# Chunk attention and a GELU layer on one core: the second tile's V loaded before the end of w_out, attention work moved into the first tile's second product, and tiles that DMA fills placed on multiples of 64 bytes

## The chip, the cores and the metric

The kernel runs on one core of a Trainium2 chip. The metric is the device time of one execution in microseconds (us). TensorE (PE) multiplies, VectorE (DVE), ScalarE (ACT) and GpSimd (POOL) do the elementwise work, and SyncE (SP) issues nearly all DMA transfers, in program order. Each engine takes its own instructions in the order in which the program lists them, and waits on semaphores for the others.

## The reference

```python
# q, k, v: (8 batches, 8 heads, 576 positions, 64); chunks of 64 positions, 9 per sequence
scores = scale * np.matmul(q_c, k_c.transpose(0, 1, 2, 4, 3))   # 64 x 64 in each chunk
attn = np.exp(scores - max); attn = attn / (attn.sum(-1) + 1e-9)
x = np.matmul(attn, v_c)            # regrouped to (4608 tokens, 512)
h = x @ w_in                        # 512 -> 2048
g = 0.5 * h * (1.0 + erf(h / sqrt(2)))
out = g @ w_out                     # 2048 -> 512, float32
```

The two products with w_in and w_out are nearly all of the arithmetic. Attention only looks within chunks of 64 positions.

## The kernel before, in words

The tokens are cut into nine tiles of 512. Tile t below 8 is the first eight chunks of batch t, and tile 8 collects the ninth chunk of every batch. For each tile there is an attention part, which gives x (128 x 4 x 512, bf16), a first product with w_in, 16 slots of four matmuls each (mm1_slot, or mm1_first for a tile's first four slots at once), each followed by Gelu on ScalarE, and a second product with w_out, 64 matmuls in blocks (phase). Everything is in bf16 with sums in float32, and the weights stay in SBUF.

The order of the work is written out by hand; nothing reorders it. From tile 2 on, q and k are transposed by DMA and the attention of tile t+1 is woven into the second product of tile t. Tiles 0 and 1 are different, because their data and the weights are still arriving: there PE transposes q and k (att_T), att_S makes the scores and their exponentials, att_av multiplies with V (a column of ones beside V gives the sum of the exponentials) and divides on DVE, and att_x transposes the result, which ScalarE or DVE copies into x. The four head pairs g of a tile go through these steps one by one.

Tile 0's second product runs by rows (mm2_rows): block f adds the products of row block f of w_out to all four output blocks, so it can start while the rest of w_out is on its way. Before the change, blocks 0 to 11 run so, and slots 12 to 15 then finish one output block each, with the last four row blocks of w_out. Tile 1's att_T and att_S stand in blocks 2 to 10, two of its att_av and one att_x in slots 14 and 15, and the other two att_av and three att_x within mm1_first of tile 1.

All loads go through one ring of seven float32 staging tiles (the tag "stage", 1 MB each) and are cast to bf16 on POOL, DVE or ScalarE. SP issues them in this order: q and k of tile 0 in eight pieces, V of tile 0 (four transfers in runs of 256 bytes), w_in in seven pieces, w_out's first quarter, q of tile 1, w_out's second quarter, k of tile 1, w_out's third and last quarters, V of tile 1 (four transfers), then q, k and V of tile 2. A quarter of w_out is four row blocks. PSUM has eight banks in three pools: mm (3), tp (2) and at (3).

The small tile act_scratch (128 x 1, float32) lies last in the pool of constants, ahead of the staging tiles; it takes a slot of 32 bytes, and in the built program the first staging tile begins at byte 59,040 of each partition, 32 past a multiple of 64. All staging tiles, the tiles of q, k and x, h and the output tiles stand at the same remainder.

Of the kernel before, what the change touches and what calls it, by code (L numbers as in the profile page):

```python
# [11 lines left out]
def kernel(  # L12
# [9 lines left out]
    nc = tc.nc  # L22
    P = 128
    f32 = mybir.dt.float32
    bf16 = mybir.dt.bfloat16
    Act = mybir.ActivationFunctionType

    B, H, S, D = q.shape
# [4 lines left out]
    G = H // 2  # L33
# [7 lines left out]
    FF = d_ff // P  # L41
    scale = 1.0 / (D ** 0.5)
# [34 lines left out]
    tiles = [dict() for _ in range(NT)]  # L77
# [51 lines left out]
    def load_v(t):  # L129
        raw = stage_tile()[:].rearrange("p (h n d) -> p h n d", h=H, d=D)  # L130
        tiles[t]["vf"] = raw
        rows_128(t, v, raw, False)

    def cast_qk(t, nm, g, copy):
        st = tiles[t]
        if t > 1 and nm == "k":
            copy(st[nm][:, :, g], st[nm + "f"][:, :, g].rearrange("p (q r) d -> p q r d", r=2))  # L137
            return
        copy(st[nm][:, g].rearrange("p j r d -> p r j d"), st[nm + "f"][:, 2 * g:2 * g + 2])  # L139

    def cast_v(t, n, copy):
        copy(v_rows[t][:, :, n, 0:D], tiles[t]["vf"][:, :, n])
# [123 lines left out]
            u = slice(half * (gs[0] % 2), half * (gs[-1] % 2 + 1))  # L266
            nc.scalar.activation(st["pT", 2 * g2 + r][:, u], st["s", g2][r][:, u], Act.Exp, scale=scale)

    def att_av(t, g, banks):

        st = tiles[t]
        half = CT // 2
        av = [pool.tile([P, half, D + 1], f32, tag=tag, name="av_ps") for pool, tag in banks]
        for n in range(half):
            for r in range(2):
                for c in range(2):
                    cs = slice(CH * c, CH * (c + 1))
                    nc.tensor.matmul(av[r][cs, n, :], st["pT", 2 * (g // 2) + r][cs, half * (g % 2) + n, :],  # L278
                                     v_rows[t][cs, 2 * g + r, n, 0:D + 1], start=True, stop=True,
                                     tile_position=(CH * c, CH * c))  # L280
        xn = work.tile([P, half, 2, D], bf16, tag="xn", name="xn", bufs=4)
        st["xn", g] = xn
        for r in range(2):
            rr = work.tile([P, half, 1], f32, tag="rr", name="rr", bufs=4)
            nc.vector.reciprocal(rr[:], av[r][:, :, D:D + 1])
            nc.vector.tensor_tensor(xn[:, :, r], av[r][:, :, 0:D], rr[:].to_broadcast([P, half, D]),  # L286
                                    op=mybir.AluOpType.mult)

    def att_x(t, g, copy, pool, tag):
        tp = pool.tile([P, CT // 2, P], bf16, tag=tag, name="tp")  # L290
        for n in range(CT // 2):
            nc.tensor.transpose(tp[:, n], tiles[t]["xn", g][:, n].rearrange("p r d -> p (r d)"), ident[:])  # L292
        copy(tiles[t]["x"][:, g, :], tp[:].rearrange("p n q -> p (n q)"))  # L293
# [4 lines left out]
    def mm1_first(t, banks, steps):  # L298
        st = tiles[t]
        st["h"] = hpool.tile([P, FF, MT], bf16, tag="h", name="h")  # L300
        h_ps = {}
        for step in steps:
            if callable(step):
                step()
                continue
            fs, kss = step
            for ks in kss:
                for f in fs:
                    if ks == 0:
                        pool, tag = banks[f]  # L310
                        h_ps[f] = pool.tile([P, MT], f32, tag=tag, name="h_ps")
                    nc.tensor.matmul(h_ps[f][:], w_in_sb[:, ks, f * P:(f + 1) * P], st["x"][:, ks, :],  # L312
                                     start=(ks == 0), stop=(ks == KS - 1))
        for f in range(len(banks)):
            nc.scalar.activation(st["h"][:, f, :], h_ps[f][:], Act.Gelu)
# [33 lines left out]
    def rows_out(t, ms):  # L349
        y_ps = tiles[t]["y_ps", ms]  # L350
        y_sb = ypool.tile([P, d_model], f32, tag="y", name="y_sb")
        (AC if t == 0 or ms < 3 and t + 1 < NT else DV)(y_sb[:], y_ps[:])  # L352
        if t == 0:
            held.append((ms, y_sb))
        elif t < B:
            store(t, ms, y_sb)
        else:
            for c in range(P // CH):
                m0 = (ms * (P // CH) + c) * S + MT
                nc.sync.dma_start(out[m0:m0 + CH, :], y_sb[c * CH:(c + 1) * CH, :])  # L360

    def last_rows(t, ms):
        h = d_model // 2
        for a, (pool, tag) in enumerate(((ps_mm, "mm"), (ps_at, "at"))):
# [6 lines left out]
            for c in range(P // CH):  # L371
                m0 = (ms * (P // CH) + c) * S + MT
                (nc.sync if c == 0 else nc.scalar).dma_start(
                    out[m0:m0 + CH, a * h:(a + 1) * h], y_sb[c * CH:(c + 1) * CH, :])

    def mm2_rows(t, f):

        last = MT // P - 1
        if f == 0:
            order = [(last, 0), (0, 0), (1, 0)]  # L380
        elif f == 1:
            order = [(last, 1), (0, 1), (1, 1), (2, 0), (2, 1)]
        else:
            order = [(ms, f) for ms in range(MT // P)]
        for ms, fi in order:
            if fi == 0:
                pool, tag = (ps_at, "at") if ms == last else (ps_mm, "mm")
                tiles[t]["y_ps", ms] = pool.tile([P, d_model], f32, tag=tag, name="y_ps")
            nc.tensor.matmul(tiles[t]["y_ps", ms][:], tiles[t]["h"][:, fi, ms * P:(ms + 1) * P], w_out_sb[:, fi, :],  # L389
                             start=(fi == 0), stop=False)  # L390

    def phase(t, extra2, by_rows=False, first=0):
        nms = MT // P
        order = [(ms, qt) for ms in range(nms) for qt in range(NQ)]
        if by_rows:
            order = [(None, f) for f in range(FF - FC)] + [(ms, NQ - 1) for ms in range(nms)]
        for f in range(first, FF):
            mm1_slot(t, f)
        for s, (ms, qt) in enumerate(order):
            for u in extra2.get(s, ()):  # L400
                u()
            if ms is None:
                mm2_rows(t, qt)
            else:
                mm2_slot(t, ms, qt)

# [16 lines left out]
            copy(w_in_sb[:, :, c * WC + i * P:c * WC + (i + 1) * P], raw[:, :, i * P:(i + 1) * P])  # L423
        return cast

    def load_w_out(c):
        raw = stage_tile()[:].rearrange("p (f n) -> p f n", f=FC)
        nc.sync.dma_start(raw, w_out_v[:, c * FC:(c + 1) * FC, :])

        def cast(i, copy):  # L430
            copy(w_out_sb[:, c * FC + i, :], raw[:, i, :])  # L431
        return cast
# [8 lines left out]
        for _ in range(n):  # L441
            nc.tensor.matmul(warm[:], rest[:, 0:P], rest[:], start=True, stop=True)

    act_scratch = consts.tile([P, 1], f32, name="act_scratch")

    def act_table(func):
        nc.scalar.activation(act_scratch[:], rest[:, 0:1], func)  # L447

    with tc.manual_schedule():
        for g in range(G):  # L450
# [7 lines left out]
        tp, at, mm = (ps_tp, "tp"), (ps_at, "at"), (ps_mm, "mm")  # L458
        for g in range(G - 1):
            cast_qk(0, "k", g, PO)  # L460
        cast_v(0, 0, PO)
        cast_qk(0, "k", G - 1, PO)
        cast_v(0, 1, PO)
        cast_v(0, 2, PO)
        for i in range(FC):
# [25 lines left out]
        att_x(0, 0, AC, *mm)  # L491
        att_av(0, 2, (at, tp))
        att_x(0, 1, AC, *mm)
        mm1_first(0, (mm, at, at, tp),
                  (((0, 1), (0,)), lambda: att_av(0, 3, (tp, at)), lambda: att_x(0, 2, AC, *mm),
                   ((0, 1), (1,)), lambda: act_table(Act.Gelu), lambda: att_x(0, 3, DV, *mm),
                   ((0, 1), (2,)), ((2, 3), (0, 1, 2)), ((0, 1, 2, 3), (3,))))
        win.append(load_w_in(NWC - 1))
        wout = [load_w_out(0)]
        load_qk(1, "q")  # L500
# [1 line left out]
        for c in range(1, NWC):  # L502
            for i in range(4):
                win[c](i, DV if i % 2 == 0 else PO)
            if c == 1:
                load_qk(1, "k")
            else:
                wout.append(load_w_out(c))
        for i in range(FC):
            wout[0](i, DV if i % 2 == 0 else PO)  # L510
        load_v(1)
        for g in range(G):
            cast_qk(1, "q", g, DV if g == 0 else PO)
        for i in range(FC):
# [2 lines left out]
            cast_qk(1, "k", g, DV if g % 2 == 0 else PO)  # L517
        for i in range(FC):
            wout[2](i, PO)
        for i in range(2):  # L520
            wout[3](i, PO)
        for n in range(CT // 2):
            cast_v(1, n, PO)

        def next_qk():
            for nm in "qk":
# [2 lines left out]
        Tq = [lambda g=g: att_T(1, "q", g, AC) for g in range(G)]  # L529
        Tk = [lambda g=g: att_T(1, "k", g, (AC, DV)[g % 2]) for g in range(G)]  # L530
        phase(0, {0: [lambda: act_table(Act.Exp)], 2: Tq[0:1], 3: Tq[1:2], 4: Tq[2:4], 7: Tk[0:2], 8: Tk[2:4],
                  9: [lambda: att_S(1, (0, 1)), next_qk], 10: [lambda: att_S(1, (2, 3)), lambda: wout[3](2, DV)],
                  11: [lambda: wout[3](3, AC)], 14: [lambda: att_av(1, 0, (at, at))],
                  15: [lambda: att_av(1, 1, (tp, tp)), lambda: att_x(1, 0, AC, *mm)]},
              by_rows=True, first=4)
        pool_cast_qk(2)
        every = (0, 1, 2, 3)
        mm1_first(1, (mm, mm, at, at),
                  (lambda: att_av(1, 2, (at, at)), (every, (0,)), lambda: att_x(1, 1, AC, *mm),
                   lambda: att_av(1, 3, (tp, tp)), (every, (1,)), lambda: att_x(1, 2, AC, *mm),  # L540
                   lambda: act_table(Act.Gelu), (every, (2,)), lambda: att_x(1, 3, DV, *tp), (every, (3,))))
        for t in range(1, NT):
            nxt = t + 1 < NT
            if nxt:
# [52 lines left out]
```

## Time and profile before

| | us |
|---|---|
| median of three runs | 294.69 (294.62 to 295.0) |
| the profiled execution's own time | 292.79 |
| its span, first to last instruction | 291.0 |
| PE busy | 277.8 (95% of the span) |
| ScalarE / DVE / POOL busy | 171.6 / 103.4 / 72.1 |
| start of tile 1's regular mm1 slots in the chain of waits | 59.01 |
| one of tiles 2 to 7, from first slot to first slot | 29.18 |

The chain of waits follows the work that ended last back to the start. It lies on PE for 91% of the span; what is not PE in it stands within the first 59 us. From there on a tile follows a tile every 29.18 us (113.90, 143.10, 172.27 and 201.44 in the chain) with PE hardly pausing.

### The profile page before, as it was taken

The page shows a single profiled execution, that of the slowest core. Times are in us where ns is not written, and L with a number is a line of the kernel's source. Part 1 is how long each engine was busy: PE and PEld are TensorE (multiplying, and loading weights), DVE is VectorE, ACT ScalarE, POOL GpSimd, SP SyncE. Part 2 cuts the span into 40 slices and gives each one's busy share as a digit, 9 for nine tenths or more (in the row PEclk, how much of TensorE's full clock was granted, in tenths as well). Part 3 has the DMA queues.
Part 4 walks back from the last instruction along what each step waited for, and adds up shares of the span by engine and source line. Part 5 has one row for each costly group of instructions (what it writes and reads, how often), then busy time and mean ns, then how long its engine had stood idle before and what let it go on. Part 6 is the DMA issues. An engine that isn't in the chain of part 4 may idle for free.

```text
span 291.0 us, 5942 instructions
## 1 busy us (share of the span) xinstructions
PE 277.8 (95%) x2401; PEld 134.2 (46%) x2431; DVE 103.4 (36%) x211; ACT 171.6 (59%) x347; POOL 72.1 (25%) x114
## 2 busy tenths in 40 slices
PE   7589999799999999999999999999999999999995
PEld 3354454444444444444444444444444444444444
DVE  2473242400940094009400950095009500950011
ACT  2547745588647864686468646864686468646400
POOL 2445565611431341053005300530006020000000
PEclk9969999999999999999999999999999999999999
DMA  7999999998879984995499539953999493030033
GB/s 235 253 346 377 364 354 240 192 237 227 221 203 222 263 181 145 215 254 113 143 212 255 116 141 207 254 124 140 197 136 146 91 235 75 2 136 8 0 74 72
DMA packets 119307, 53.87 MB, mean 185 GB/s; under 512 B 97648, under 2 KB 112240, under 8 KB 119280
## 3 DMA queue, kind: packets, MB, share of 16 engines
q1 hardware_dynamic: 119120, 53.36, 75.9%
q8 instruction: 19, 0.31, 0.5%
q10 hardware_dynamic: 160, 0.13, 0.2%
q14 instruction: 8, 0.07, 0.1%
HBM read 36.70 MB, written 9.44 MB: 159 GB/s over the span
## 4 chain that ended last, share of the span: by engine, by line
PE 91%; SPq 3%; DMA 2%; DVE 1%; issue 1%; ACT 1%
PE h_ps L323 40%; PE y_ps L338 38%; PE y_ps L389 3%; PE h_ps L312 3%; PE av_ps L236 2%; PE s_ps L184 2%; DMA arrival<-in_v_dram 2%; SPq L100 2%; SPq L90 1%; PE y_ps L367 1%; PE tp L292 1%; PE av_ps L278 1%; PE tp L148 1%; DVE xn L286 1%; ACT x L293 0%
## 5 line engine op out<-in xcount | busy, mean ns | idle before, releaser
L323 PE MATMUL h_ps<-x,w_in_sb 128*128 128x512 bf16 x535 | 118.4, 379 | 0.5
L325 ACT ACTIVATE h<-h_ps 128x512 bf16<-128x512 f32 x136 | 81.0, 598 | 59.3 <-PE h_ps L323 59.3
L338 PE MATMUL y_ps<-w_out_sb,h 128*128 128x512 bf16 x496 | 111.4, 379 | 1.5 <-issue 1.1
L323 PEld LDWEIGHTS <-w_in_sb 128*128 128x128 bf16 x544 | 53.2, 98 | 64.2
L338 PEld LDWEIGHTS <-h 128*128 128x128 bf16 x512 | 48.8, 98 | 57.4
L202 DVE STREAM_TRANSPOSE pt<-pT 128x256 f32<-128x256 f32 x28 | 12.2, 437 | 108.6 <-ACT pT L191 108.6
L139 POOL CAST q_nat<-arrival 128x512 bf16<-128x512 f32 x31 | 18.0, 621 | 96.2 <-DMA arrival<-in_q_dram 63.5
L162 POOL CAST v_nat<-arrival 128x1024 bf16<-128x1024 f32 x14 | 14.5, 1040 | 39.9 <-DMA arrival<-in_v_dram 30.6
L447 ACT ACT_TABLE_LOAD x18 | 23.1, 1283 | 1.0 <-PEq L581 0.7
L215 ACT COPY part<-part 32x32 f32<-32x32 f32 x56 | 12.3, 219 | 15.1 <-DVE part L205 14.6
L243 DVE TENSOR_TENSOR x<-av_ps,rc 128x512 bf16<-128x512 f32 x28 | 18.9, 676 | 2.2
L205 DVE TENSOR_REDUCE part<-pt 128x16 f32<-128x512 bf16 x28 | 19.2, 686 | 1.0
L352 DVE COPY y_sb<-y_ps 128x512 f32<-128x512 f32 x10 | 6.9, 691 | 34.9 <-PE y_ps L338 34.9
L137 POOL CAST k_nat<-arrival 128x512 bf16<-128x512 f32 x28 | 16.6, 613 | 5.8 <-DMA arrival<-in_k_dram 5.6
L352 ACT COPY y_sb<-y_ps 128x512 f32<-128x512 f32 x25 | 14.5, 580 | 3.3 <-PE y_ps L338 2.4
L191 ACT ACTIVATE pT<-s_ps 128x512 bf16<-128x512 f32 x28 | 14.3, 593 | 0.0
L389 PE MATMUL y_ps<-w_out_sb,h 128*128 128x512 bf16 x46 | 11.6, 380 | 0.1
L312 PE MATMUL h_ps<-x,w_in_sb 128*128 128x512 bf16 x30 | 8.6, 403 | 1.5 <-ACT x L293 1.0
L229 DVE STREAM_TRANSPOSE rc<-rb 128x512 f32<-128x512 f32 x14 | 9.9, 707 | 0.2
L229 DVE STREAM_TRANSPOSE rc<-across 128x512 f32<-128x512 f32 x14 | 9.8, 702 | 0.0
L423 POOL CAST w_in_sb<-arrival 128x512 bf16<-128x512 f32 x10 | 7.1, 729 | 7.6 <-DMA arrival<-in_moe_w_in_dram 7.6
L431 POOL CAST w_out_sb<-arrival 128x512 bf16<-128x512 f32 x10 | 6.9, 727 | 4.0 <-DMA arrival<-in_moe_w_out_dram 4.0
(52 smaller groups left out, 140.8 us busy)
## 6 DMA issues: line engine op xcount, KB each, us to landing
out_dram<-y_sb SPq DMA_DIRECT2D x32, 256.0 KB, 2.4
arrival<-in_k_dram SPq DMA_DIRECT2D x28, 256.0 KB, 6.5
arrival<-in_q_dram SPq DMA_DIRECT2D x7, 1024.0 KB, 6.8
arrival<-in_v_dram SPq DMA_DIRECT2D x42, 128.0 KB, 3.1
arrival<-in_moe_w_out_dram SPq DMA_DIRECT2D x4, 1024.0 KB, 14.1
arrival<-in_moe_w_in_dram SPq DMA_DIRECT2D x6, 512.0 KB, 8.0
arrival<-in_v_dram SPq DMA_DIRECT2D x8, 256.0 KB, 6.7
arrival<-in_v_dram SPq DMA_DIRECT2D x28, 64.0 KB, 2.7
```

What stands on the lines that cost most here:

```text
L137: copy(st[nm][:, :, g], st[nm + "f"][:, :, g].rearrange("p (q r) d -> p q r d", r=2))
L139: copy(st[nm][:, g].rearrange("p j r d -> p r j d"), st[nm + "f"][:, 2 * g:2 * g + 2])
L205: nc.vector.tensor_reduce(st["part", g2][:, c, :, :, 0], pt[:].rearrange("p n e u -> p n u e"), axis=mybir.AxisListType.X, op=mybir.AluOpT ...
L229: nc.vector.transpose(rc[:], tiles[t]["rb", g2][c].to_broadcast([P, NB, 32]))
L243: nc.vector.tensor_tensor(x.rearrange("p n (e u) -> p n e u", u=2), st["av"][g2][c][:].rearrange("p n (e u) -> p n e u", u=2), st["rc", 2 ...
L312: nc.tensor.matmul(h_ps[f][:], w_in_sb[:, ks, f * P:(f + 1) * P], st["x"][:, ks, :], start=(ks == 0), stop=(ks == KS - 1))
L323: nc.tensor.matmul(h_ps[:], w_in_sb[:, ks, f * P:(f + 1) * P], st["x"][:, ks, :], start=(ks == 0), stop=(ks == KS - 1))
L325: nc.scalar.activation(st["h"][:, f, :], h_ps[:], Act.Gelu)
L338: nc.tensor.matmul(y_ps[:], st["h"][:, f, ms * P:(ms + 1) * P], w_out_sb[:, f, :], start=(f == 0), stop=(f == FF - 1))
L352: (AC if t == 0 or ms < 3 and t + 1 < NT else DV)(y_sb[:], y_ps[:])
L389: nc.tensor.matmul(tiles[t]["y_ps", ms][:], tiles[t]["h"][:, fi, ms * P:(ms + 1) * P], w_out_sb[:, fi, :], start=(fi == 0), stop=False)
L447: nc.scalar.activation(act_scratch[:], rest[:, 0:1], func)
```

## The change

It has these parts.

- act_scratch becomes 128 x 32 float32, so that the first staging tile begins at byte 59,136, a multiple of 64, and all that follows it likewise. The reciprocals rr of one att_av share one tile.
- At the start, POOL casts the last piece of k of tile 0 ahead of the first piece of V, not behind it.
- Tile 0's last att_av (g = 3) stands before mm1_first, not within it, and its second multiply, one DVE instruction before, becomes four ScalarE instructions with a scale per partition.
- V of tile 1 is loaded ahead of w_out's last quarter, and that quarter comes in two halves. Its four casts go to DVE (12), POOL (13 and 15, behind the V casts) and ScalarE (14).
- Tile 0's second product runs by rows up to block 13; four short blocks 14 to 17 of two matmuls finish the output blocks. Tile 1's four att_av stand at blocks 12, 13, 15 and 17 and two of its att_x at 14 and 15; two att_x stay in mm1_first, which works by all four slots at once, over other PSUM banks. The copies of tile 0's third and fourth output blocks move into mm1_first.

```diff
-    def att_av(t, g, banks):
+    def att_av(t, g, banks, second=None):
...
+        rr = work.tile([P, 2, half, 1], f32, tag="rr", name="rr", bufs=4)
         for r in range(2):
-            rr = work.tile([P, half, 1], f32, tag="rr", name="rr", bufs=4)
-            nc.vector.reciprocal(rr[:], av[r][:, :, D:D + 1])
-            nc.vector.tensor_tensor(xn[:, :, r], av[r][:, :, 0:D], rr[:].to_broadcast([P, half, D]),
-                                    op=mybir.AluOpType.mult)
+            nc.vector.reciprocal(rr[:, r], av[r][:, :, D:D + 1])
+            if r == 0 or second is None:
+                nc.vector.tensor_tensor(xn[:, :, r], av[r][:, :, 0:D], rr[:, r].to_broadcast([P, half, D]),
+                                        op=mybir.AluOpType.mult)
+            else:
+                for n in range(half):
+                    nc.scalar.activation(xn[:, n, r], av[r][:, n, 0:D], Act.Copy, scale=rr[:, r, n])
...
+    FR = FF - 2
+
+    def mm2_last(t, ms):
+        y_ps = tiles[t]["y_ps", ms]
+        for f in range(FR, FF):
+            nc.tensor.matmul(y_ps[:], tiles[t]["h"][:, f, ms * P:(ms + 1) * P], w_out_sb[:, f, :],
+                             start=False, stop=(f == FF - 1))
+        if ms < 2:
+            rows_out(t, ms)
...
-            order = [(None, f) for f in range(FF - FC)] + [(ms, NQ - 1) for ms in range(nms)]
+            order = [(None, f) for f in range(FR)] + [(ms, None) for ms in range(nms)]
...
-    def load_w_out(c):
+    def load_w_out(c, parts=1):
...
+        n = FC // parts
+        for a in range(parts):
+            nc.sync.dma_start(raw[:, a * n:(a + 1) * n], w_out_v[:, c * FC + a * n:c * FC + (a + 1) * n, :])
...
-    act_scratch = consts.tile([P, 1], f32, name="act_scratch")
+    act_scratch = consts.tile([P, 32], f32, name="act_scratch")
...
-        cast_v(0, 0, PO)
         cast_qk(0, "k", G - 1, PO)
+        cast_v(0, 0, PO)
...
+        att_av(0, 3, (tp, at), AC)
         mm1_first(0, (mm, at, at, tp),
-                  (((0, 1), (0,)), lambda: att_av(0, 3, (tp, at)), lambda: att_x(0, 2, AC, *mm),
-                   ((0, 1), (1,)), lambda: act_table(Act.Gelu), lambda: att_x(0, 3, DV, *mm),
-                   ((0, 1), (2,)), ((2, 3), (0, 1, 2)), ((0, 1, 2, 3), (3,))))
+                  (((0, 1), (0,)), lambda: att_x(0, 2, AC, *mm), ((0, 1), (1,)), lambda: act_table(Act.Gelu),
+                   lambda: att_x(0, 3, DV, *mm), ((0, 1), (2,)), ((2, 3), (0, 1, 2)), ((0, 1, 2, 3), (3,))))
...
-                wout.append(load_w_out(c))
+                if c == NWC - 1:
+                    load_v(1)
+                wout.append(load_w_out(c, 2 if c == NWC - 1 else 1))
...
-        load_v(1)
...
-        for i in range(2):
-            wout[3](i, PO)
         for n in range(CT // 2):
             cast_v(1, n, PO)
+        for i in (1, 3):
+            wout[3](i, PO)
...
-                  9: [lambda: att_S(1, (0, 1)), next_qk], 10: [lambda: att_S(1, (2, 3)), lambda: wout[3](2, DV)],
-                  11: [lambda: wout[3](3, AC)], 14: [lambda: att_av(1, 0, (at, at))],
-                  15: [lambda: att_av(1, 1, (tp, tp)), lambda: att_x(1, 0, AC, *mm)]},
+                  9: [lambda: att_S(1, (0, 1)), next_qk], 10: [lambda: att_S(1, (2, 3)), lambda: wout[3](0, DV)],
+                  12: [lambda: att_av(1, 0, (at, at))], 13: [lambda: att_av(1, 1, (tp, tp)), lambda: wout[3](2, AC)],
+                  14: [lambda: att_x(1, 0, AC, *at)],
+                  15: [lambda: att_av(1, 2, (at, tp)), lambda: att_x(1, 1, AC, *tp)],
+                  17: [lambda: att_av(1, 3, (at, mm))]},
...
-        mm1_first(1, (mm, mm, at, at),
-                  (lambda: att_av(1, 2, (at, at)), (every, (0,)), lambda: att_x(1, 1, AC, *mm),
-                   lambda: att_av(1, 3, (tp, tp)), (every, (1,)), lambda: att_x(1, 2, AC, *mm),
-                   lambda: act_table(Act.Gelu), (every, (2,)), lambda: att_x(1, 3, DV, *tp), (every, (3,))))
+        mm1_first(1, (mm, at, tp, mm),
+                  (lambda: att_x(1, 2, AC, *mm), (every, (0,)), lambda: rows_out(0, 2), lambda: att_x(1, 3, DV, *tp),
+                   lambda: rows_out(0, 3), (every, (1,)), lambda: act_table(Act.Gelu), (every, (2, 3))))
```

More of the change, by code (lines that the diff above doesn't have):

```diff
@@ L403, in phase @@
                 mm2_rows(t, qt)
+            elif qt is None:
+                mm2_last(t, ms)
             else:
@@ L424, in load_w_in @@
         return cast
-    def load_w_out(c):
+    def load_w_out(c, parts=1):
         raw = stage_tile()[:].rearrange("p (f n) -> p f n", f=FC)
-        nc.sync.dma_start(raw, w_out_v[:, c * FC:(c + 1) * FC, :])
+        n = FC // parts
+        for a in range(parts):
+            nc.sync.dma_start(raw[:, a * n:(a + 1) * n], w_out_v[:, c * FC + a * n:c * FC + (a + 1) * n, :])
         def cast(i, copy):
@@ L442, in keep_warm @@
             nc.tensor.matmul(warm[:], rest[:, 0:P], rest[:], start=True, stop=True)
-    act_scratch = consts.tile([P, 1], f32, name="act_scratch")
+    act_scratch = consts.tile([P, 32], f32, name="act_scratch")
     def act_table(func):
-        nc.scalar.activation(act_scratch[:], rest[:, 0:1], func)
+        nc.scalar.activation(act_scratch[:, 0:1], rest[:, 0:1], func)
     with tc.manual_schedule():
@@ L460 @@
             cast_qk(0, "k", g, PO)
+        cast_qk(0, "k", G - 1, PO)
         cast_v(0, 0, PO)
-        cast_qk(0, "k", G - 1, PO)
         cast_v(0, 1, PO)
```

## The prediction

> **What bounds the kernel now.** I read the page first, then the chain of waits in order of time, then the timelines of PE, POOL, DVE and ScalarE over the first 62 us, and last the table by windows.
>
> ```profile
> PE 277.8 (95%) x2401; PEld 134.2 (46%) x2431; DVE 103.4 (36%) x211; ACT 171.6 (59%) x347; POOL 72.1 (25%) x114
> ```
>
> PE bounds the whole. So only time in which PE waits can be won, and the chain of waits shows where that is (start, length, what):
>
> ```profile
> 9.47 4.65 DMA arrival<-in_v_dram
> 14.12 0.02 issue
> 14.15 0.44 DVE v_rows L142
> ...
> 47.31 1.51 PE y_ps L338 x7
> 48.82 0.15 issue
> 48.97 0.44 PE av_ps L278 x16
> ...
> 53.66 0.59 ACT x L293
> 54.26 0.04 issue
> 54.30 1.02 PE h_ps L312 x4
> ...
> 59.01 1.51 PE h_ps L323 x7
> ```
>
> Three things are to be seen. At the start, PE cannot go on before the last piece of V lands at 14.1. Between 47.31 and 59.01 the chain leaves PE for three copies of x (53.66 is the first; 55.58 and 57.50 are alike). After 59.01 it stays on PE until the end. The second place is also where transfers end, as POOL's timeline shows (start, length):
>
> ```profile
> 41.77 2.29 POOL L431 CAST w_out_sb<-arrival 128x512 bf16<-128x512 f32 x4 [1.09 <-DMA arrival<-in_moe_w_out_dram]
> 44.59 1.43 POOL L431 CAST w_out_sb<-arrival 128x512 bf16<-128x512 f32 x2 [0.55 <-DMA arrival<-in_moe_w_out_dram]
> 45.97 1.17 POOL L142 CAST v_rows<-arrival 128x512 bf16<-128x512 f32 x2
> 47.65 0.61 POOL L142 CAST v_rows<-arrival 128x512 bf16<-128x512 f32 x1 [0.52 <-DMA arrival<-in_v_dram]
> 48.48 0.61 POOL L142 CAST v_rows<-arrival 128x512 bf16<-128x512 f32 x1 [0.21 <-DMA arrival<-in_v_dram]
> ```
>
> w_out's third quarter lands at about 41.75, its last at 44.55, V's last piece at 48.45: 2.8 us for a quarter of w_out, 3.9 for V, as much data each. The last V cast ends at 49.09, so the first att_av of tile 1 could hardly stand earlier than its slot 14.
>
> **Part 1: tile 1's attention in the second product.** From 47.31 to 59.01 are 11.70 us. PE's own work there, from its rows: four att_av at 0.37 (1.48), 16 matmuls of the second product at 0.86 a group of four (3.44), four transposes of x at 0.24 (0.96), 16 first-product matmuls (3.44): 9.32. So 2.38 are waits: 0.15 for V, about 0.65, 0.65 and 0.50 for three copies of x, and three refills of 0.16 (a group of four reads 1.02 behind a wait and 0.86 otherwise).
>
> Afterwards all this work stands in another order, and I follow it with the same durations.
> - V now queues where w_out's last quarter was. If the queue serves in order of issue, as all casts above began in that order, V ends at 48.45 - 2.8 = 45.65 and the halves of w_out land at 47.05 and 48.45. POOL's V casts end at about 46.3; PE reaches the first att_av at 47.3. Cover 1.0.
> - Row block 12: DVE casts it from 47.05 to 47.65 (0.59). PE arrives at 47.7; I take 0.1. Block 13: POOL to 47.9, needed at 49.0. Block 14: ScalarE from 48.45 to 49.1 (0.62), needed at 50.1. Block 15: POOL to 49.1.
> - Behind these waits: on DVE the reciprocals of the first att_av, ready only at 47.7; on ScalarE the copy of the first x, ready at 50.1; on POOL the casts of tile 2's q, whose data came at 53.1. None is held longer than before. On SP the halves are one transfer more, about 0.6 us of issue, ahead of tile 2's q. The same bytes precede that q, so I cost this at nothing.
> - The first two x now have two short blocks and an att_av between transpose and use: their copies (0.59) are hidden. The output copies stand between them on ScalarE, which ends its second one at about 52.5; the third x's transpose wants that bank at 52.8. Cover 0.3, the thinnest.
> - One stall stays. In the built program the third x is transposed into PSUM bank 2, and the first matmul of tile 1's first product writes the same bank. PE must wait for ScalarE's copy: 0.65 and a refill of 0.16.
> - The copies of the third and fourth output blocks and the table load (1.28 + 0.20) follow on ScalarE to about 56.3; the first Gelu is wanted at 56.9.
>
> Left are 0.1 + 0.81 = 0.91; saved is 2.38 - 0.91 = 1.47. Tile 2 then needs its transposed k 1.5 us sooner, at 67.9 for 69.37; that transfer is issued at 60.46 and lands in 4.6, at 65.1. Its V is cast by 71.3 and wanted at 74.7. So the gain is kept.
>
> **Part 2: the start.** k's last cast, behind V's first (10.96) now, moves ahead of it, and its transposes (12.19) come about 1 us sooner. PE waits after that for V's last piece all the same, which DVE casts at 14.15: no gain.
>
> The early att_av(3) puts its DVE work right behind that of g = 2, which ends at 18.53 (before: a gap to 19.32). Two reciprocals and one multiply end at about 19.3. Then four ScalarE instructions of 64 elements, which no row shows. The groups by shape that come near (busy us, mean ns of one | idle):
>
> ```profile
> L191 ACT ACTIVATE pT<-s_ps 128x512 bf16<-128x512 f32 x28 | 14.3, 593 | 0.0
> L215 ACT COPY part<-part 32x32 f32<-32x32 f32 x56 | 12.3, 219 | 15.1 <-DVE part L205 14.6
> ...
> L267 ACT ACTIVATE pT<-s_ps 128x256 bf16<-128x256 f32 x8 | 2.6, 381 | 2.7 <-PE s_ps L262 2.7
> ```
>
> The bounds are 219 ns (32 elements) and 381 (256); neighbours overlap by about 0.1 (two of 381 took 0.66). 64 is nearest 32: 4 x 0.22 = 0.88, to 20.2. The copy of x(2) waits behind these on ScalarE: to 20.8 plus 0.05, where PE resumes; it was 20.96. Gain 0.1. With 0.58 in all it is 0.3, after which PE's own work binds; with 1.52, 0.5 is lost.
>
> The Trainium skill ("ScalarE: Activation LUTs", rules for kernel authors) speaks against this step: it sends multiplies to VectorE. Its formula gives (as an estimate) 332 ns for 64 elements with one pointer operand, less 93 of overlap, so 1.05 us for four, and this step would gain nothing; the sum would be 1.5 in place of 1.6.
>
> **Part 3: multiples of 64.** Every load and store moves from 32 past a multiple of 64 to 0. A table by windows compares V of tile 0 (runs of 256 bytes) with w_out (2,048); the last three figures are clock, DMA share, GB/s:
>
> ```profile
> 10.90:14.10 3.20, 1.61 (x45) 0.94 (x35) 0.35 (x1) 1.63 (x5) 2.40 (x4) 0.88 1.14 223
> 30.30:33.30 3.00, 2.95 (x14) 1.37 (x14) 1.18 (x3) 2.01 (x4) 1.62 (x2) 1.00 1.07 374
> ```
>
> Both land at the same remainder, so 374 GB/s is possible with it, and V's 223 goes with its short runs. I take zero. The other bound is V at w_out's rate: 1.05 MB in 2.8 us for 4.7, a gain of 1.9 at the start, which the earlier k would then just allow (att_av from 12.6 on, for 14.63). A loss is excluded: whatever was on a multiple of 32 still is.
>
> "DMA: Bandwidth & Descriptors" (how a descriptor splits into AXI transactions) says that a start off a 256-byte boundary costs extra beats. The first staging tile moves from 160 past such a boundary onto one; if that held for writes into SBUF, a 256-byte run would need 8 beats for 13 (an estimate), and the sum would be near the 1.9 bound. No row here shows it.
>
> **Sum.** 1.47 + 0.1 = 1.6 us. The profiled execution took 292.79 (span 291.0 and 1.8 around it) and would take 291.2. The median of the runs stands 1.9 above it; the saved waits are no share of that, so 294.69 - 1.6 = 293.1.
>
> **Rivals.**
> - *The boundary of 64 speeds the short runs.* For it: with 16 DMA engines busy (share 1.14), V moved only 223 GB/s, so each run has a cost of its own, and alignment could be in it. Against it: 374 at the same offset. Price up to 1.9 more: 291.2. TensorE's clock stood at 0.50 from about 13.3 to 20.1; should more work there keep it up, some 0.3 more.
> - *w_out's end comes late: slower.* V's four issues held SP for 11.8 us (33.28 to 45.04) before; both halves of w_out are now issued behind them and are the next thing that the second product needs. The earlier place of V brings the last issue to about 43.9. If a half then takes the 8.0 us of w_in's halves from issue to landing, it lands at 51.9, PE waits for block 12 until 52.5 rather than 47.7, and the sum is 4.8 lost against 1.6 won: 297.9. It decides at a landing of 48.7, 1.6 after my 47.05. Against it: the 8.0 were spent behind a full queue, and here the share is 0.88 to 1.10 while it drains.
> - *The bank stall and the output copies cost more.* If the third x also waits for its bank (cover 0.3), or its copy behind an output copy (0.58), two such waits take 1.2: 294.3, no change that can be told.
>
> **How the numbers follow.** My forecast 0.50, the faster start 0.24, no change 0.09, w_out late 0.17. A measurement tells about 0.2% (0.6 us) from no change. Faster by more than that is 0.74, within it 0.09, slower 0.17. The range goes from 291.0 (all of the 1.9, and a little of the clock) to 294.7 (the third rival and a little); w_out late stays outside. My forecast's own range is 292.4 to 293.9.
>
> **What would show it.** Right: no wait for V before the first att_av of tile 1; the regular mm1 slots of tile 1 begin at 57.4 in the chain; one copy of x (0.6) is left in it ahead of them; PE resumes at about 20.9 in the start; V's last cast of tile 0 still at 14.1. If that comes at 12.5 to 13.5, the boundary works. Wrong: DVE or PE waits for w_out at block 12 beyond 48.7; ScalarE's four multiplies above 1.2 us; or the gain at 57.4 is lost at tile 2's scores, where k must be there by 67.9.

## The result, and the profile after

The changed kernel took 293.18 us (median of four runs, 293.06 to 293.43) beside 294.81 for the kernel before in the same session: ratio 0.9946, interval 0.9929 to 0.9963. The forecast was 293.1. That is 1.6 us less [1.1 to 2.1]. Later the changed kernel was measured once more, at 0.997 [0.995, 0.999], 0.9 us less [0.3 to 1.5]; the experiments say of what the gain is made. Its profiled execution took 293.06 us with a span of 291.3.

The busy times of after, as the page gives them (us, share of the span, instructions):

```profile
PE 280.4 (96%) x2431; PEld 134.1 (46%) x2431; DVE 102.8 (35%) x210; ACT 172.1 (59%) x351; POOL 71.4 (25%) x114
```

The chain of waits of after, with the places that were shown of before (start, length, what):

```profile
9.18 5.52 DMA arrival<-in_v_dram
...
14.72 0.44 DVE v_rows L142
...
21.68 3.24 PE h_ps L316 x12
24.92 10.36 PE h_ps L327 x48
...
46.85 1.83 PE y_ps L403 x8
48.68 0.37 PE av_ps L278 x16
49.05 0.97 PE y_ps L403 x4
...
54.48 0.24 PE tp L296 x4
54.72 0.02 issue
54.74 0.59 ACT x L297
...
55.38 1.02 PE h_ps L316 x4
56.40 0.22 PE tp L296 x4
56.63 2.59 PE h_ps L316 x12
```

Block 11 of tile 0's second product ends at 48.68. Where before's chain had three copies of x, one is left (54.74). Tile 1's regular slots begin at 59.22, 10.54 us after block 11; before they began 11.70 us after it. After that a tile takes 29.17 us (114.11, 143.28 and 172.46 in the chain), as before. The absolute 59.22 is later than before's 59.01 all the same, because the start of this execution is 1.4 us later (tile 0's regular slots at 24.92). That is not the change's work alone, and it is the first thing that the experiments had to untangle.

POOL's timeline of after shows the loads in their new order (start, length, line, what, and what ended the idle time before):

```profile
38.97 2.29 POOL L449 CAST w_out_sb<-arrival 128x512 bf16<-128x512 f32 x4 [0.94 <-DMA arrival<-in_moe_w_out_dram]
41.20 1.73 POOL L142 CAST v_rows<-arrival 128x512 bf16<-128x512 f32 x3
43.98 0.61 POOL L142 CAST v_rows<-arrival 128x512 bf16<-128x512 f32 x1 [1.05 <-DMA arrival<-in_v_dram]
46.17 0.87 POOL L449 CAST w_out_sb<-arrival 128x512 bf16<-128x512 f32 x1 [1.58 <-DMA arrival<-in_moe_w_out_dram]
47.46 0.61 POOL L449 CAST w_out_sb<-arrival 128x512 bf16<-128x512 f32 x1 [0.42 <-DMA arrival<-in_moe_w_out_dram]
```

V's last piece is cast from 43.98 and the halves of w_out from 46.14 (row block 12, by VectorE) and 47.46; PE wants the first half at 49.05. Nothing waits for w_out.

### The profile page after: what moved, and what is told of

Read it like the earlier page. It is cut to its first block, busy times and chain, and to the rows that moved or that the text cites. A ratio compares the mean times of both kernels' runs of the same rounds, so it can differ in the third digit from the quotient of the medians.

```text
span 291.3 us, 5973 instructions
## 1 busy us (share of the span) xinstructions
PE 280.4 (96%) x2431; PEld 134.1 (46%) x2431; DVE 102.8 (35%) x210; ACT 172.1 (59%) x351; POOL 71.4 (25%) x114
## 3 DMA queue, kind: packets, MB, share of 16 engines
q1 hardware_dynamic: 119136, 53.36, 69.5%
## 4 chain that ended last, share of the span: by engine, by line
PE 93%; SPq 3%; DMA 2%; DVE 1%; ACT 1%; issue 0%
PE h_ps L327 40%; PE y_ps L342 37%; PE y_ps L403 4%; PE h_ps L316 3%; DMA arrival<-in_v_dram 2%; PE av_ps L236 2%; PE s_ps L184 2%; SPq L100 1%; SPq L90 1%; PE y_ps L371 1%; PE tp L296 1%; PE av_ps L278 1%; PE y_ps L385 1%; PE tp L148 1%; ACT pT L267 0%; PE s_ps L262 0%
## 5 line engine op out<-in xcount | busy, mean ns | idle before, releaser
L342 PEld LDWEIGHTS <-h 128*128 128x128 bf16 x496 | 47.4, 98 | 55.8
L297 ACT COPY x<-tp 128x512 bf16<-128x512 bf16 x6 | 3.5, 588 | 9.2 <-PE tp L296 9.2
```

What stands on the lines that cost most here:

```text
L342: nc.tensor.matmul(y_ps[:], st["h"][:, f, ms * P:(ms + 1) * P], w_out_sb[:, f, :], start=(f == 0), stop=(f == FF - 1))
```

## Experiments: why the profiled execution of before was 1.9 us under its own median

The kernel before was run once more, unchanged, with three others beside it.

> The kernel before, unchanged, to get a second profiled execution of it: the one shown took 292.79 us, while the runs read 294.6 to 295.0, and the changed kernel's profiled execution took 293.06 like its runs. Theory 1 (the start differs from execution to execution): this execution takes about 294.7, and the 1.9 us more stand before 24 us in the chain of waits, in the landing of V's last piece (14.1 in the one shown) or in a longer stretch at half of TensorE's clock. Theory 2 (the second tile's attention differs): the 1.9 more stand between 47 and 59 us. Theory 3: the span is 291.0 again and the runs differ outside the span.

Measured: 294.81 us, ratio 0.9996 [0.9974, 1.0018]; its profiled execution took 294.49, span 292.7. From its chain:

```profile
15.32 0.44 DVE v_rows L142
...
44.62 5.46 DMA arrival<-in_v_dram
...
50.13 0.63 POOL v_rows L142
```

Two loads explain it. V's last piece of tile 0 was cast at 15.32 instead of 14.15, and V's last piece of tile 1 at 50.13 instead of 48.48, so that the chain leaves PE for that transfer and the stretch from block 11 to tile 1's slots is 12.1 us instead of 11.70: 1.2 + 0.4 of the 1.7 us of span. So the shown execution of before was a lucky one in both places.

All profiled executions of this study can be put side by side by three numbers: when V's last piece of tile 0 is cast, how long it takes from there to tile 0's first regular slot, and how long from the end of block 11 to tile 1's.

| kernel | V cast at | to tile 0's slots | block 11 to tile 1's slots |
|---|---|---|---|
| before | 14.15 | 9.40 | 11.70 |
| before, again | 15.32 | 9.43 | 12.1 |
| before, aligned (multiple of 256) | 15.87 | 10.03 | 11.69 |
| before, multiple of 64 only | 15.54 | 9.55 | 12.0 |
| tile 1's part alone | 15.18 | 9.60 | 10.54 |
| after, not aligned | 16.57 | 10.29 | 10.54 |
| after | 14.72 | 10.20 | 10.54 |
| after, again | 15.30 | 10.32 | 10.53 |
| after, other banks | 14.35 | 9.33 | 9.79 |
| after, fill matmuls | 15.07 | 9.00 | 10.53 |
| after, plain copies | 16.49 | 10.15 | 10.53 |
| both edits, plain copies | 15.96 | 8.99 | 9.80 |
| both, VectorE multiply, plain copies | 14.72 | 8.26 | 11.45 |

The first column varies by 2.4 us with no order in it: single executions can't be compared by their ends, only stretch by stretch. What sets the landing of that last piece was not found.

## Experiments: the three parts one by one

**Alignment alone.** The kernel before with the larger scratch tile and nothing else:

```diff
-    act_scratch = consts.tile([P, 1], f32, name="act_scratch")
+    act_scratch = consts.tile([P, 32], f32, name="act_scratch")
...
-        nc.scalar.activation(act_scratch[:], rest[:, 0:1], func)
+        nc.scalar.activation(act_scratch[:, 0:1], rest[:, 0:1], func)
```

> The kernel before with only act_scratch widened to 32 elements, so that all tiles stand on multiples of 64 bytes. My forecast (the offset does nothing): the time of the kernel before, ratio 0.999 to 1.001, w_out's third quarter lands at 41.7 as before. Rival (aligned rows move faster, as the changed kernel's trace hints with 393 to 410 GB/s for 367 to 385): the third quarter lands at about 39.0; and either V's first landing comes sooner too and the time falls by 0.5 to 1.9 us (ratio 0.9935 to 0.998), or only the long rows gain, PE waits for none of them, and the time stays within 0.3 us.

Measured: 294.17 us, ratio 0.9988 [0.9969, 1.0007]: no gain that can be told, as forecast. Yet the transfers did change, as the last part of the rival had it. The queue that carries the loads, in the kernel before and, behind it, in the aligned one (packets, MB, share of 16 engines' span):

```profile
q1 hardware_dynamic: 119120, 53.36, 75.9%
```

```profile
q1 hardware_dynamic: 119120, 53.36, 68.9%
```

The same packets took less time. The traces with 119,120 or 119,136 packets agree: 68.9 to 70.4% in the five with the large scratch tile, 75.0 to 77.2% in the five others, that of the next experiment among them. POOL's casts of w_out's first three quarters in the aligned kernel:

```profile
29.27 1.61 POOL L431 CAST w_out_sb<-arrival 128x512 bf16<-128x512 f32 x2 [0.95 <-DMA arrival<-in_moe_w_out_dram]
34.56 1.61 POOL L431 CAST w_out_sb<-arrival 128x512 bf16<-128x512 f32 x2 [0.57 <-DMA arrival<-in_moe_w_out_dram]
39.83 2.29 POOL L431 CAST w_out_sb<-arrival 128x512 bf16<-128x512 f32 x4 [0.95 <-DMA arrival<-in_moe_w_out_dram]
```

From quarter to quarter (with q or k of tile 1 between them, 2 MB) are 5.29 and 5.27 us; in the kernel before 5.71 and 5.72 (30.34, 36.05, 41.77). So rows of 2,048 bytes and q's and k's came 8% faster. No gain shows for V's runs of 256 bytes: its last piece of tile 0 was cast at 15.87, and V of tile 1 took 4.5 us from w_out's end (42.42 to 46.93), where the three traces of this order off the boundary have 3.9, 5.2 and 4.9. The start waits for V, and PE doesn't wait for w_out, so what is won is not on the path.

**64 or 256.** The new place, 59,136, is a multiple of 256 as well. One execution of the kernel before with a scratch tile of 64 bytes, which puts the staging tiles at 59,072, on a multiple of 64 and 192 past one of 256:

```diff
+    act_scratch = consts.tile([P, 16], f32, name="act_scratch")
```

> The kernel before with act_scratch at 16 elements: the first staging tile at byte 59,072, a multiple of 64 that is 192 past a multiple of 256, where 32 elements put it on a multiple of 256 too. Theory 1 (64 bytes decide): w_out's quarters land every 2.55 to 2.75 us, as with 32 elements, 5 to 7% faster than the 2.7 to 3.0 of the kernel before, in its first landings 2 us ahead by the third quarter. Theory 2 (256 bytes decide, by extra beats at each boundary): rates as in the kernel before.

Measured: 294.67 us. The share of that queue and POOL's casts of w_out's first three quarters:

```profile
q1 hardware_dynamic: 119120, 53.36, 76.5%
```

```profile
31.19 1.62 POOL L431 CAST w_out_sb<-arrival 128x512 bf16<-128x512 f32 x2 [1.16 <-DMA arrival<-in_moe_w_out_dram]
36.87 1.62 POOL L431 CAST w_out_sb<-arrival 128x512 bf16<-128x512 f32 x2 [0.81 <-DMA arrival<-in_moe_w_out_dram]
42.51 2.29 POOL L431 CAST w_out_sb<-arrival 128x512 bf16<-128x512 f32 x4 [1.08 <-DMA arrival<-in_moe_w_out_dram]
```

The steps are 5.68 and 5.64 us, as without any alignment. So a multiple of 64 does nothing here, and a multiple of 256 is enough; a multiple of 128 that is not one of 256 was not tried. "DMA: Bandwidth & Descriptors" of the Trainium skill (how a descriptor splits into AXI transactions) has the boundary of 256: a piece that starts off a multiple of 256 bytes costs extra beats. The page tells it of what a transaction reads; here the place written to in SBUF was moved. The long rows behave so (8%), and the gain that the rule would give for runs of 256 bytes does not show.

**All but the alignment.** The changed kernel with the small scratch tile put back (the first diff of this section, reversed).

> The changed kernel with act_scratch back at one element: all its parts but the alignment. My forecast: the same 1.6 us below the kernel before as the whole change (ratio 0.9946), block 12 of the second product waits at most 0.1 us for w_out. Rival (the alignment carries it): w_out's last quarter lands 1 us or more later than the 46.1 of the changed kernel, PE waits at block 12, and the ratio is 0.997 or more.

Measured: 293.89 us, 0.9974 [0.9954, 0.9994]; 10.54 us from block 11 to tile 1's slots. The ratio is the rival's, but its mechanism did not come: w_out's first half was cast from 49.49, and PE came to block 12 at 50.99 without waiting. What else makes the ratio so is not shown; this execution has the latest V of tile 0 in the table.

**Tile 1's part alone.** The same, and the start as it was before:

```diff
-        cast_qk(0, "k", G - 1, PO)
         cast_v(0, 0, PO)
+        cast_qk(0, "k", G - 1, PO)
...
-        att_av(0, 3, (tp, at), AC)
         mm1_first(0, (mm, at, at, tp),
-                  (((0, 1), (0,)), lambda: att_x(0, 2, AC, *mm), ((0, 1), (1,)), lambda: act_table(Act.Gelu),
...
+                  (((0, 1), (0,)), lambda: att_av(0, 3, (tp, at)), lambda: att_x(0, 2, AC, *mm),
...
```

> The kernel before with only the second tile's part: V ahead of w_out's last quarter in two halves, the att_avs from block 12 on, the new mm1_first of tile 1; no alignment, and the start as before. My forecast: 1.47 us less than the kernel before (ratio 0.995), the stretch from the end of block 11 to the regular slots of tile 1 takes 10.2 us for 11.7. Rival (the moved work saves less, since the changed kernel's trace reads 10.5): 1.2 us (ratio 0.996), and the rest of the whole change comes from the start.

Measured: 293.55 us, 0.9968 [0.9945, 0.9991], and 10.54 us in the stretch, as the rival had it. This kernel and the one above it differ in the start alone: 293.55 with the old start, 293.89 with the new one. No gain of the new start shows; 0.1 us is less than these runs can tell. The alignment's rows (0.9988 alone; 0.9974 without it against 0.9946 and 0.997 with it) put it at 0.4, 0.8 and 0.1 us, and their intervals allow zero. Tile 1's part carries the gain: 0.0032 x 294.5 = 0.9 us [0.3 to 1.6].

## Experiments: what is left in the two stretches

The changed kernel was run again beside two variants of it.

> The changed kernel, unchanged, beside the kernel before in the same rounds, and as the base of the two kernels that follow. Six profiled executions so far put the landing of V's last piece in tile 0 anywhere from 14.1 to 16.6 us, whatever the kernel, and every one with the second tile's part reads 10.54 us between block 11 and tile 1's regular slots for 11.70 without. Theory 1 (one fixed saving of 1.2 us, and an execution's start is luck): ratio 0.996 to the kernel before. Theory 2 (the alignment takes away a further wait for V of tile 1, which a late execution of the kernel before shows at 50.1 us): ratio 0.9945 to 0.995.

Measured: 293.32 us, 0.997 [0.995, 0.999]; stretch 10.53. That is nearer to theory 1, and the interval just reaches theory 2.

**The bank.** Tile 1's third and fourth x go through other banks, and the third no longer through the one that the first matmul of mm1_first writes:

```diff
-                  (lambda: att_x(1, 2, AC, *mm), (every, (0,)), lambda: rows_out(0, 2), lambda: att_x(1, 3, DV, *tp),
+                  (lambda: att_x(1, 2, AC, *tp), (every, (0,)), lambda: rows_out(0, 2), lambda: att_x(1, 3, DV, *at),
```

> The changed kernel with tile 1's third x transposed into a bank of the tp pool and its fourth into one of the at pool, so that the first matmul of tile 1's first product no longer writes the bank that ScalarE still reads. Theory (the stall named in the forecast, 0.65 us and a refill of 0.16, is that bank alone): from block 11 to the regular slots 9.7 us for 10.54, no copy of x in the chain there, and 0.8 us less in the time. Rival (another wait takes its place: the first x's copy or a Gelu): 10.3 us or more.

Measured: 292.01 us, 0.9916 [0.9893, 0.9938]. Its chain:

```profile
47.44 0.37 PE av_ps L278 x16
47.80 0.97 PE y_ps L403 x4
...
52.70 0.54 PE y_ps L385 x2
53.24 0.22 PE tp L296 x4
53.46 0.96 PE h_ps L316 x4
54.42 0.22 PE tp L296 x4
54.64 2.59 PE h_ps L316 x12
```

The copy of x is out of the chain, the stretch is 9.79 (47.44 to 57.23), 0.74 less than beside it, as the theory had it. The median fell by 1.31, more than that. Part of it is the clock: TensorE's mean granted clock is on record for every run, and between the runs with 0.986 to 0.988 (four here, 292.14 us; eight of the changed kernel, 292.88) the difference is 0.7. The chain also shows what remains over PE's own 9.32: a group of four matmuls behind an att_av takes 0.97 and two take 0.54, where 0.86 and 0.43 are the rule. So a return from the 64 x 65 matmuls of att_av to full ones costs 0.11. The four behind the last transposes take 0.96; what that comes from is not shown.

**The clock.** PE stands still while it waits for V, and the table by windows of after gives, in its last three figures, clock, DMA share and GB/s:

```profile
13.00:17.00 4.00, 0.80 (x24) 0.68 (x23) 1.86 (x7) 0.00 (x0) 1.02 (x2) 0.88 1.04 346
17.00:20.00 3.00, 3.00 (x44) 1.93 (x43) 2.46 (x10) 1.41 (x4) 1.94 (x4) 0.50 1.09 385
20.00:24.00 4.00, 4.00 (x19) 2.03 (x18) 2.18 (x5) 2.65 (x7) 2.12 (x3) 0.64 1.07 403
```

PE is busy for 0.80 of 4 us, and then works at half clock without a pause. In windows of 1 us the clock is 1.00 up to 16, 0.52 in the next and 0.50 from 17 on. The edit gives it matmuls of no use during the wait:

```diff
+        keep_warm(12)
         att_av(0, 0, (tp, tp))
         att_av(0, 1, (at, at))
+        keep_warm(3)
```

> The changed kernel with 12 matmuls on zeros (2.6 us) ahead of tile 0's first att_av, where TensorE waits for V, and 3 more ahead of the first transpose of x. Theory 1 (the early att_av and ScalarE's multiplies gained nothing in tile 0 because TensorE's clock stands at 0.50 from its pause on, so that TensorE's own work binds): the clock stays at 1.00, from V's landing to the first regular slot it takes 9.1 us for 10.2, and the time falls by 1.1 us (ratio to the changed kernel 0.996). Rival (the attention's chain on DVE and ScalarE binds): 9.8 us or more, and at most 0.4 less in the time.

Measured: 292.4 us, 0.9934 [0.9912, 0.9956], 0.9 us less than the changed kernel beside it. The same windows:

```profile
13.00:17.00 4.00, 3.81 (x46) 1.76 (x44) 1.55 (x6) 0.32 (x2) 1.05 (x2) 1.00 0.99 305
17.00:20.00 3.00, 2.62 (x48) 1.59 (x48) 2.66 (x11) 1.31 (x3) 2.02 (x5) 1.00 1.01 343
20.00:24.00 4.00, 3.64 (x18) 1.67 (x18) 1.90 (x5) 3.29 (x9) 2.00 (x4) 1.00 1.06 369
```

The clock stays at 1.00, and from V's cast to tile 0's slots are 9.00 us for 10.2 to 10.3. "TensorE: Matmul & The Clock Gate" of the Trainium skill (HAM oscillation) asks for no pause of PE above some 3.4 us. Here less was enough: in after the longest pause in that place was 2.24 us, followed by 0.50 us of small matmuls, and the clock fell at 16.05, 0.35 us into the next pause; in before it fell at 13.32, and the longest pause in the 3.41 us ahead of that was 1.20 us. So what counted here was little work over some time, not one long pause. With the fill it stayed.

Windows of 0.1 us over the first 30 us show more. In the ten traces in which the clock falls, it stays at half for 3.41 us (after, other banks), 10.24 us (tile 1's part alone; after, plain copies) or 6.83 us (all others): one, three or two times 3.41. In the 3.41 us ahead of each fall PE was busy for 0.50 to 1.89 us. Once fallen, the clock stayed at half behind every stretch of 3.41 us with at most 3.00 us of work and came back behind the first with 3.06 or more. This also orders the times of the changed kernel: its eight runs with a mean clock of 0.988 have a median of 292.88 us, its four with 0.982 to 0.983, which comes to 10.2 us at half, 294.63. The kernel before, in the same rounds, has 294.17 and 294.76. So the change wins 1.3 us in the first group and 0.1 in the second; this sorts runs that were there, and no run set the length by itself. Against the first group the fill wins 0.6 us (292.26, its five runs at 0.998 and above).

**Both, and ScalarE's multiplies.** Three more kernels were run together. In all three, the transposing transfers of q and k of tiles 2 to 8 are plain copies of the same bytes, so they compare among themselves: the changed kernel, the one with both edits, and that one with the last multiply of the early att_av back on VectorE.

```diff
-        nc.sync.dma_start_transpose(st[nm + "t"][:], st[nm][:].rearrange("p g j r d -> p (g j r d)"))
+        nc.sync.dma_start(st[nm + "t"][:].rearrange("p a b -> p (a b)"), st[nm][:].rearrange("p g j r d -> p (g j r d)"))
```

> The base for the two kernels beside it: the changed kernel with the transposing transfers of q and k of tiles 2 to 8 turned into plain copies of the same bytes. The transposition of those tiles is left out, so what is computed from tile 2 on is not the reference's; tiles 0 and 1 are computed as before. Theory (PE binds after 59 us, 29.17 us a tile, and nothing of tile 2's q and k is on the chain): the time of the changed kernel, 293.2 to 293.4 us, ratio to the kernel before 0.995 to 0.997, 10.5 us from the end of block 11 to tile 1's slots. Rival (the copies are quicker or slower enough to be seen): outside 292.3 to 294.3 us.

Measured: 293.07 us, 0.9948 [0.993, 0.9965]; 10.53 in the stretch. The copies don't show, as the theory had it.

> The base beside it (transposition of q and k of tiles 2 to 8 left out in the same way) with the fill matmuls at the start and the two x of tile 1 in other PSUM banks. Theory (two separate waits, each on the chain): both gains add. At the start 6.4 us from V's last landing to the group of 12 matmuls for 6.9 in the base, granted clock 0.99 or more, 9.0 to the first regular slot of tile 0 for 9.3 to 10.2; 9.80 us from the end of block 11 to tile 1's slots for 10.54. Together 0.9 for the clock and 0.75 for the bank: 1.6 us under the base beside it, some 291.6. Rival (the gains of the two single runs were in part an early landing of V): 1.0 us or less under the base.

Measured: 291.77 us, 0.9907 [0.9888, 0.9926], 1.30 under the base, between the theory's 1.6 and the rival's 1.0; the stretches are those of the theory, 9.80 and 8.99, with a clock of 1.000. Its start, from the chain:

```profile
20.62 0.10 DVE rr L285
20.75 0.93 ACT xn L291 x4
21.68 0.48 ACT x L297
22.16 0.04 issue
22.20 2.75 PE h_ps L316 x12
```

With the clock full, PE waits for ScalarE: four multiplies, and the copy of x queued behind them. That is what the third kernel takes away.

```diff
-        att_av(0, 3, (tp, at), AC)
+        att_av(0, 3, (tp, at))
```

> As the kernel with both edits (transposition of q and k of tiles 2 to 8 left out in the same way), with the last multiply of the early att_av of tile 0 back on VectorE: one of 0.42 us there for 0.93 of ScalarE's four. Theory (with the clock full, PE no longer binds here and the chain goes over ScalarE's multiplies and the copy of x queued behind them: with the fill matmuls they ran from 19.86, that copy from 20.66 to 21.26, and PE's group of 12 from 21.32): the copy starts once its transposes are done (19.7), VectorE ends the multiply at 20.3, and the group of 12 starts at about 20.7; 5.8 us from V's landing to it for 6.43, and about 0.6 us less in time than the kernel beside it. Rival (ScalarE's step pays, because VectorE is the engine that binds there): 6.4 us or more, and the time of the kernel beside it or above.

Measured: 291.55 us, 0.9896 [0.9874, 0.9918]; only 0.2 under the kernel beside it, within the intervals. The stretch that the theory spoke of did shrink, from 8.99 to 8.26 us. But PE's timeline then shows two waits that no kernel with this order of loads had before it:

```profile
46.67 0.38 PE L278 MATMUL av_ps<-v_rows,pT 64*64 64x65 bf16 x12
47.73 0.25 PE L278 MATMUL av_ps<-v_rows,pT 64*64 64x65 bf16 x4 [0.68 <-POOL v_rows L142]
48.78 1.02 PE L403 MATMUL y_ps<-w_out_sb,h 128*128 128x512 bf16 x4 [0.80 <-DVE w_out_sb L449]
```

V's last piece landed at 47.06 and w_out's first half at 48.30, and PE, earlier by now, stood at both: 11.45 us for 9.80. What the start wins, the loads take back, in the profiled execution. This is the forecast's late w_out, which did not come with the change. PE is not its only cause: V came 6.5 us behind w_out's third quarter here and at most 5.2 in the other traces with the new order. Whether these waits return in the other executions was not seen.

## Why the prediction was right, point by point

- **The place of the gain** was right: tile 1's part alone gives 0.9968, and the chain lost two of three copies of x. The stall at the third x was there, 0.65 and 0.16, and moving its bank took away 0.74.
- **Its size was too large**, a term of the sum. 1.47 was forecast and 1.16 measured against the shown execution (11.70 to 10.54). PE's timeline of before shows, in brackets, what PE waited for in the stretch:

```profile
54.30 1.02 PE L312 MATMUL h_ps<-x,w_in_sb 128*128 128x512 bf16 x4 [0.30 <-ACT x L293]
...
56.22 1.02 PE L312 MATMUL h_ps<-x,w_in_sb 128*128 128x512 bf16 x4 [0.67 <-ACT x L293]
...
57.98 1.02 PE L312 MATMUL h_ps<-x,w_in_sb 128*128 128x512 bf16 x4 [0.52 <-DVE x L293]
```

  These are 1.49 us, and with three refills 1.97, where the forecast had 2.38. The step that failed is the sum of PE's own work, 9.32, made with 0.86 for every group of four: before's own chain reads 0.97 behind an att_av (at 49.41), and 0.33 for four transposes behind one (at 50.74). PE's own time was 9.73, so 0.41 of the 2.38 was never a wait. In the list of waits, the first copy of x was priced at 0.65 and cost 0.30, because the fourth att_av ran meanwhile (at 53.56). The 0.15 was no wait for V: its row has 7 of 8 matmuls, and 1.51 and 0.15 are 1.66, where eight take 1.73; the aligned kernel's chain has the same 0.15 at 51.17, and there V's last cast began at 46.93. After waits 0.67 for one copy, with a refill of 0.16, and its own time is 9.71: the waits fell by 1.14. The wait for w_out's block 12, 0.1, did not come (it was cast from 46.14, not 47.05). Against the executions in which V of tile 1 came late (two of the four with the old order of loads) the part saves 1.5 to 1.6.
- **The new start, 0.1**, does not show. The four multiplies took 0.93 against 0.88 forecast; one took 314 ns. But what binds at half clock is PE: in after's chain all from 16.71 on is PE, so the earlier end on DVE and ScalarE buys nothing. Once the clock is full, the step is a loss in its stretch: 8.99 for 8.26. "ScalarE: Activation LUTs" of the Trainium skill (rules for kernel authors), which sends such multiplies to VectorE and by which 1.05 and no gain had been estimated, was the better guide here. In four of five executions with the new start and no fill the half clock reached into the group of 12 matmuls (3.24 for 2.59 in after), in one of five with the old one; whether the new start causes that was not tried by itself. The part of the forecast that failed is that it costed the start by DVE and ScalarE while PE, at half clock, was the longer path.
- **Alignment at zero** was right for the time and wrong for the reason. The forecast argued that a rate of 374 GB/s was possible off the boundary, and so that nothing was to be won. The long rows did gain 8%; they are not on the path.
- **The execution to subtract from.** The forecast took 1.6 off the median as well as off the lucky execution. The median is 1.6 less; the profiled execution was to take 291.2 and took 293.06. So of the signs named, the absent wait for V (the shown execution of before had none either) and the one copy of x that is left came, and the times did not: 59.22 for 57.4, 21.68 for 20.9, 14.72 for 14.1.
- **That 293.18 came within 0.1 of 293.1 is in part luck.** The stretch gives 1.16, up to 1.6 where V is late. The four runs of the first measurement all had a clock of 0.987 or 0.988; with four of twelve at 0.982 to 0.983 the second gave 0.9 us, and the variant with plain copies 1.5.
- **The rivals.** The late w_out did not come with the change (49.05 is when PE wants it, and it was cast from 46.14). The faster start did not either: V's last cast was at 14.72, and from 14.35 to 16.57 in the variants. The dearer bank and output copies did not: one stall of 0.81, as in the forecast, not two for 1.2.

## What to carry to other kernels

Compare two executions stretch by stretch, from an event to an event on the path, before reading a difference of their ends: here one load's landing varied by 2.4 us, more than the whole change. Where PE binds after a wait, it pays for the wait again in work at half clock, and matmuls of no use in the wait won 0.9 us here and cost nothing (0.76 us from V's last cast to the first reciprocal, with them and without); cost elementwise shortcuts only after that, since they may turn from free to binding. When a stall at a PSUM bank is seen in the built order, another bank is worth trying first (0.74 us for two names).

## What was not expected of the hardware

- A load into SBUF of long rows is 8% faster from a multiple of 256 bytes (5.29 for 5.71 us per 2 MB) and not at all from a multiple of 64 that is 192 past one of 256 (5.68).
- V's last piece of tile 0 was cast anywhere from 14.15 to 16.57 us, and V of tile 1 took 3.9 to 6.5 us behind the quarter of w_out ahead of it. What sets this was not found.
- A return from the matmuls of 64 x 65 to full ones costs 0.11 us (0.97 for 0.86 a group of four).
- TensorE's clock fell to half with no pause above 1.20 us in the 3.41 us ahead of it (before, at 13.32), and it stays at half for 3.41, 6.83 or 10.24 us: in after from 16.05 to 22.87, although PE works without a pause from 17 on.
